# A recurrent attention loop and a long convolution on one core: one arena for the working tiles, a smaller descriptor ring, 13 streamed weight blocks, and loads moved to SyncE

## The chip, the cores and the metric

The kernel runs on one core of a Trainium2 chip. The metric is the device time of one execution, in microseconds; three executions of the kernel before took 2227.32, 2236.9 and 2243.41 us, median 2236.9.

The engines named below are TensorE (PE; its weight loads are PEld), VectorE (DVE), ScalarE (ACT), GpSimd (POOL) and SyncE (SP). SP and POOL also issue DMA transfers, each in its own program order.

## The reference

The output is two halves side by side, 2048 rows each of 1024 columns in bf16.

```python
# half A: 64 segments of 32 rows, one after the other
mem = mem0                                        # [1, 8, 1024]
for s in range(64):
    h = concat([mem, x[:, 32*s:32*s + 32]], 1)    # 40 rows
    q, k, v = (einsum('btd,dhe->bhte', h, W) for W in (Wq, Wk, Wv))   # 32 heads of 128
    scores = einsum('bhqe,bhke->bhqk', q, k) * 128 ** -0.5
    scores = where((idx[:, None] < 8) | (idx[:, None] >= idx[None, :]), scores, -1e9)
    o = einsum('bhqk,bhke->bhqe', softmax(scores), v)
    o = einsum('bhte,hed->btd', o, Wo)
    mem = o[:, :8]                                # carried to the next segment
    outs.append(o[:, 8:])
# half B: a state-space convolution along the 2048 rows
K = einsum('dn,dnl,dn->dl', C, exp(dt * A * l), dt * B).real
y = irfft(rfft(pad(u)) * rfft(pad(K)))[:2048] + u * Dskip
```

The recurrence through `mem` makes the 64 segments of half A sequential. Each needs all of Wq, Wk, Wv and Wo, 64 blocks of 128 x 2048 bf16 (512 KB each), which are more than SBUF holds.

## The kernel before

**Order of the whole.** Half B runs first (0 to about 721 us): tables of powers, spectra of u and of K by matrix products, a pointwise complex product, and inverse products. In its shadow the parts of half A that don't depend on `mem` are projected ahead (keys, queries and values of the 24 rows a segment that come from x alone), kept in DRAM in `PKd`, `PVd` and `XTd`, and weight blocks are loaded into SBUF as rooms come free. Then comes the loop over segments in `part_a` (about 721 to 2150 us), then one product for the left-over rows of all segments, to the end.

**Half B, pointwise stage.** A loop `for b in range(16)` over column quarters `dq = b // 4` and frequency chunks `b % 4`. Each turn does a spectrum of K by matrix products (`spectrum(b + 1)`, L1010), the complex product on DVE (`pointwise(b)`, L1184 to L1195, ten operations), and the issue of the spectrum of u for two turns later (`load_u(b + 2)`, L984, on SP). At b = 0 it also issues `load_k` for the last two quarters (L957): each is 31 small DMAs that gather rows of `Kd`, the key table in DRAM, into `KT2`. From b = 4 on, each turn does two inverse products (L1242) with `load_inverse` (u rows `uu`, L1202) and the store of the result. In the kernel before, POOL issues these key loads, the `uu` loads and the stores.

**A segment.** The state is `hT`, 32 columns for each of eight row groups: 24 from x and 8 from `mem`. Heads are in two halves t = 0, 1. `quads(m, t, kcs)` multiplies `hT` by the blocks of k, q or v (L348), four column groups at once. `evac` copies the result to SBUF on ACT (L354), `tr` transposes it (L359), `scores` makes q times k with the rows of the segment and the 24 rows left of it as two halves of one PSUM tile `sc` of 128 x (2 x 4 x 40). The softmax is two functions over the whole tile, `softmax_a` (largest, subtraction, exponential on ACT) and `softmax_b` (sum, reciprocal, product, two transposes), L389 to L399. `spread` and `spread_l` set the probabilities out in blocks for the next product (`pb`, `lb`, L404 and L407, DVE), and `left_blocks` those of the left rows (`L`, POOL). `pv_x` multiplies v by them; `oproj` (L450) multiplies by the 16 blocks of Wo; `pv_l` is the same product for the left rows. `ob` is the segment's result, half copied by DVE, half by ACT (L540, L541); `tro` transposes it and DVE writes it into `hT` (L546), which releases the next segment.

**Order of work in a segment.** The loop is under `tc.manual_schedule()`: each engine takes its instructions in the order of the text, and waits come from the use of tiles. `between[key]` hangs an extra step (loading `pk`, storing `ob`, fetching a kept block) just before the block `key` is asked for.

**Where weights lie.** Most blocks stay in SBUF (`W_res`). `STREAM` and `STREAM_O` name 14 that `unit` loads afresh in every segment from a DRAM copy `WD` into a ring `wst` of five slots, on SP; a load waits for the matmuls that read the slot last. Two more, (k, 0, 7) and (o, 15), lie in four PSUM banks (`KEPT`, `load_kept`); `fetch` copies them to SBUF in five pieces each with DVE (L283). `SCRATCH` is the SBUF area that holds the ring of descriptors of the DMAs that POOL issues: 2048 bytes a partition; the rest of that area holds `Wlow` blocks.

**Working tiles.** They come from a pool `work` under tags A, B, C, E, F, L and mx; a tag's room is as large as its largest tile, and several tiles share a tag in turn. `pk` (768 wide: kl, ql, vl) and `xt` (192 wide: the next rows of x) are loaded by SP each segment.

Of the kernel before, what the change touches and what calls it, by code (L numbers as in the profile page):

```python
# [24 lines left out]
STREAM = {("k", 0): (1,), ("q", 0): (0, 6), ("k", 1): (3,), ("q", 1): (0, 5), ("v", 0): (2, 7), ("v", 1): (2, 7)}  # L25
STREAM_O = (3, 6, 9, 13)

BANK = {("k", 0): "b0", ("q", 0): "b1", ("k", 1): "b2", ("q", 1): "b0", ("v", 0): "b3", ("v", 1): "b2"}
KEPT = {("k", 0, 7): (("B", 0, 512), ("C", 512, 512), ("A", 1024, 512), ("F", 1536, 256), ("L", 1792, 256)),
        ("o", 15): (("B", 0, 512), ("C", 512, 512), ("E", 1024, 512), ("F", 1536, 256), ("L", 1792, 256))}  # L30
SLOTS = 5

# [33 lines left out]
class Ahead:  # L66
# [3 lines left out]
    def __init__(self, ctx, tc, x, src, seg_len):  # L70
# [5 lines left out]
        self.XTd = dram.tile([self.NS, 128, self.KC * self.XM], BF16, name="XTd")  # L76
        self.PKd = dram.tile([self.NS, 128, 768], BF16, name="PKd")
# [7 lines left out]
    def transposes(self, pool, ps, ident):  # L85
# [7 lines left out]
        for b in range(self.S // 128):  # L93
# [10 lines left out]
            nc.sync.dma_start(out=self.XTd[4 * b:4 * b + 4].rearrange("s p f -> p s f"), in_=xst[:].rearrange("p s k r -> p s (k r)"))  # L104
            yield

    def projections(self):

        nc, KC, NS, XL, PKd, xTl = self.nc, self.KC, self.NS, self.XL, self.PKd, self.xTl
# [13 lines left out]
        def rows_out(t):  # L123
            for k in range(XL):
                late.append(lambda k=k, t=t: nc.sync.dma_start(out=PKd[:].rearrange("s (h k) f -> k s h f", k=XL)[k][:, :, 512 + 128 * t:640 + 128 * t],
                                  in_=self.PVd[t][:].rearrange("(s k) (h e) -> k s h e", k=XL, e=128)[k]))
# [53 lines left out]
def constants(tc, const, ahead):  # L180
# [3 lines left out]
    ident = const.tile([128, 128], BF16, name="a_ident")  # L184
    make_identity(nc, ident[:])
    mask = const.tile([128, 2, NK], BF16, name="mask")
    nc.gpsimd.memset(mask[:], 0.0)
    BD = const.tile([128, 4], BF16, name="BD")
    BDx = ahead.low[2]
    BDL = const.tile([128, 4, 4], BF16, name="BDL")  # L190
# [15 lines left out]
    hT = const.tile([128, ahead.KC, SL], BF16, name="hT")  # L206
# [23 lines left out]
def part_a(ctx, tc, x, src, WD, HE, seg_len, out_a, ahead, W_res, rest, places, first):  # L230
# [13 lines left out]
    XTd, PKd, OLd = ahead.XTd, ahead.PKd, ahead.OLd  # L244
    ident, mask, BD, BDx, BDL, hT = ahead.consts

# [10 lines left out]
    def unit(key):  # L257
# [6 lines left out]
        if key in KEPT:  # L264
            return ahead_of.pop(key)
# [3 lines left out]
        t_ = wst.tile([128, 2048], BF16, name="wst", tag="w%d" % (loads[0] % SLOTS))  # L269
        loads[0] += 1  # L270
        nc.sync.dma_start(out=t_[:], in_=WD[key][:])
        return t_
# [3 lines left out]
    work = ctx_l.enter_context(tc.tile_pool(name="a_work", bufs=1))  # L276
    ps = ctx_l.enter_context(tc.tile_pool(name="a_ps", bufs=1, space=PSUM))
    ps_k = ctx_l.enter_context(tc.tile_pool(name="a_keep", bufs=1, space=PSUM))
    kept, ahead_of = {}, {}
    pn, pt = ahead.low[0:2]  # L280
# [3 lines left out]

    def load_kept(key):
        i = len(kept)
        if key in first:
            t_ = first.pop(key)
        else:
            t_ = wst.tile([128, 2048], BF16, name="wst", tag="w%d" % (loads[0] % SLOTS))  # L290
            loads[0] += 1
            nc.sync.dma_start(out=t_[:].rearrange("e (h d) -> e h d", h=2) if key[0] == "o" else t_[:], in_=src(key))
        kept[key] = [ps_k.tile([128, 512], F32, name="keep", tag="keep%d" % (2 * i + n)) for n in range(2)]
        for n in range(2):
            words(kept[key][n][:], t_[:, 1024 * n:1024 * n + 1024])

    def fetch(key):

        ahead_of[key] = []
        for tag, lo, n in KEPT[key]:  # L300
            t_ = work.tile([128, n], BF16, name="piece", tag=tag)
            words(t_[:], kept[key][lo // 1024][:, lo % 1024 // 2:(lo % 1024 + n) // 2])
            ahead_of[key].append((lo, n, t_))
# [7 lines left out]
    def load_pk(j):  # L311
        pk = pers.tile([128, 768], BF16, name="pk", tag="pk")
        nc.sync.dma_start(out=pk[:], in_=PKd[j])
# [1158 lines left out]
```

## Time and profile before

| what | value |
|---|---|
| median of three executions | 2236.9 us |
| profiled execution, its time | 2233.63 us |
| its span, first to last instruction | 2231.9 us |
| busy: PE, DVE, ACT, POOL | 1908.5, 1400.5, 1025.5, 510.1 us |
| DMA moved | 657.84 MB |
| 63 copies into hT (L546), first and last start | 760.7 and 2136.0 us |

By stage, busy time of each engine with its DMA share and rate:

| stage, us | PE | DVE | ACT | POOL | DMA share | GB/s |
|---|---|---|---|---|---|---|
| half B, tables (0 to 478) | 369.4 | 420.1 | 403.0 | 194.0 | 0.73 | 199 |
| half B, products (478 to 721) | 225.0 | 212.1 | 71.8 | 95.5 | 0.65 | 217 |
| first segment (721 to 761) | 25.1 | 14.9 | 9.6 | 4.0 | 0.96 | 348 |
| the other segments (761 to 2136) | 1211.3 | 737.6 | 526.4 | 201.6 | 0.96 | 350 |
| end (2136 to 2232) | 77.8 | 15.8 | 14.7 | 15.0 | 0.41 | 150 |

How to read what follows. L12 is line 12 of the kernel. A row of a timeline has the start, the duration, engine, line, operation and tiles, and in brackets how long the engine had been idle and what ended that. A row of the table of waits has the total, the number and the longest. A DMA's row on SPq or POOLq is only its issue; the data land later. Busy time on an engine that isn't waited for costs nothing.

### The profile page before, as it was taken

To read this page: it belongs to the slowest core of one execution; us is meant where nothing else is said; L and a number is where in the kernel's file an instruction comes from. 1 tells how busy PE (TensorE), PEld (TensorE's weight loads), DVE (VectorE), ACT (ScalarE), POOL (GpSimd) and SP (SyncE) were. 2 spreads that over 40 slices of the span, in tenths; PEclk is the share of its full clock that TensorE was granted. 3 is DMA by queue.
4 is the path that set the end of the run, shared out by engine and by line. 5 is a ranking of instruction groups with operands and counts; after the bars stand their busy time and mean duration, and the time that the engine had idled before them with its cause. 6 is when DMAs were issued, how large, how long until landed. Compare 5 with 4: busy or idle time off the path is not lost.

```text
span 2231.9 us, 77710 instructions
## 1 busy us (share of the span) xinstructions
PE 1908.5 (86%) x33645; PEld 1181.8 (53%) x33670; DVE 1400.5 (63%) x2904; ACT 1025.5 (46%) x1727; POOL 510.1 (23%) x880
## 2 busy tenths in 40 slices
PE   1599999878999788888888988888889888889879
PEld 1365666657887354554545544544445554544434
DVE  8599999989996455555555545555545554545440
ACT  6699999941333333434343434343334333334330
POOL 2154443566222111111111111111111111111130
PEclk9999999989999899999999999999999999999989
DMA  6877786567458999999999999999999999999981
GB/s 161 195 201 231 220 239 189 158 166 274 151 178 299 342 370 354 355 356 351 359 350 355 361 337 335 359 345 355 342 351 351 362 356 344 344 346 331 362 326 29
DMA packets 351883, 657.84 MB, mean 295 GB/s; under 512 B 118616, under 2 KB 209912, under 8 KB 349492
## 3 DMA queue, kind: packets, MB, share of 16 engines
q1 hardware_dynamic: 336324, 608.69, 78.4%
q0 software_dynamic: 15216, 44.18, 5.8%
q8 instruction: 264, 4.33, 0.8%
q14 instruction: 79, 0.65, 0.1%
HBM read 597.97 MB, written 66.31 MB: 298 GB/s over the span
## 4 chain that ended last, share of the span: by engine, by line
PE 39%; DMA 26%; DVE 17%; issue 10%; ACT 5%; POOL 2%; SPq 2%; ACTq 0%; DVEq 0%; POOLq 0%
PE acc L348 18%; DMA wst<-WD_o 9%; DMA wst<-WD_q 8%; PE pp L450 4%; PE pe L574 2%; DMA wst<-WD_v 2%; PE pro L159 2%; PE tr L359 2%; DVE nr L1071 2%; DMA out_dram<-uu 2%; PE ups L869 2%; PE pa L1040 2%; DMA KT<-Kd 1%; ACT E L1048 1%; DVE mx L395 1%
## 5 line engine op out<-in xcount | busy, mean ns | idle before, releaser
L348 PEld LDWEIGHTS <-hT 128*32 128x32 bf16 x12352 | 341.3, 97 | 331.4 <-issue 103.2
L354 ACT CAST ev<-acc 128x512 bf16<-128x512 f32 x384 | 225.1, 586 | 316.2 <-PE acc L348 310.6
L348 PE MATMUL acc<-W,hT 128*32 128x512 bf16 x4864 | 349.3, 382 | 0.8 <-issue 0.8
L348 PE MATMUL acc<-wst,hT 128*32 128x512 bf16 x2560 | 261.0, 387 | 18.8 <-DMA wst<-WD_q 10.2
L450 PEld LDWEIGHTS <-oT 128*32 128x32 bf16 x8192 | 203.5, 97 | 120.6 <-issue 104.5
L283 DVE TENSOR_SCALAR piece<-keep 128x256 int32<-128x256 int32 (+1 forms) x640 | 189.3, 363 | 93.7 <-PE pp L450 91.9
L366 POOL COPY KT<-pk 128x128 bf16<-128x128 bf16 x128 | 37.6, 294 | 743.3 <-PE acc L348 388.6
L471 DVE COPY KT<-tr 128x512 bf16<-128x512 bf16 x64 | 27.2, 425 | 261.0 <-PE tr L359 261.0
L450 PE MATMUL pp<-W_o,oT 128*32 128x256 bf16 x4096 | 183.9, 277 | 5.1 <-DMA W_o<-in_A_Wo_dram 5.1
L412 POOL TENSOR_TENSOR L<-low_pt,BD 128x128 bf16<-128x128 bf16 x128 | 66.3, 518 | 463.8 <-DVE low_pt L399 236.0
L348 PE MATMUL acc<-MF,hT 128*32 128x512 bf16 x2048 | 170.0, 379 | 0.0
L437 ACT CAST oT<-pv 128x512 bf16<-128x512 f32 x128 | 75.3, 589 | 167.5 <-PE pv L423 167.2
L450 PE MATMUL pp<-wst,oT 128*32 128x256 bf16 x2048 | 102.5, 277 | 37.2 <-DMA wst<-WD_o 36.2
L541 ACT CAST ob<-pp 128x128 bf16<-128x128 f32 x64 | 17.0, 266 | 231.0 <-DVE ob L540 231.0
L159 PE MATMUL pro<-xTl,wsl 128*128 128x512 bf16 x493 | 117.6, 385 | 6.4 <-ACT xTl L103 5.2
L391 ACT ACTIVATE sc<-sc 128x320 f32<-128x320 f32 x128 | 54.0, 422 | 145.4 <-DVE sc L390 115.3
L1010 PEld LDWEIGHTS <-MF 128*128 128x128 bf16 x1024 | 102.4, 100 | 30.9 <-issue 9.8
L389 DVE TENSOR_REDUCE mx<-sc 128x8 f32<-128x320 f32 x128 | 62.2, 486 | 85.9 <-PE sc L382 85.8
L419 PEld LDWEIGHTS <-ev 128*128 128x128 bf16 x1024 | 51.3, 97 | 114.7 <-issue 101.6
L395 DVE TENSOR_REDUCE mx<-sc 128x8 f32<-128x320 f32 x128 | 63.0, 492 | 74.2 <-ACT sc L391 74.2
L1010 PE MATMUL hps<-KT,MF 128*128 128x256 bf16 x720 | 93.8, 282 | 15.7 <-DVE x L1185 12.6
L1242 PE MATMUL yp<-Bt,MI 128*128 128x256 bf16 x680 | 102.8, 273 | 0.8 <-ACT yb L1258 0.8
(315 smaller groups left out, 4011.2 us busy)
## 6 DMA issues: line engine op xcount, KB each, us to landing
wst<-WD_q SPq DMA_DIRECT2D x256, 512.0 KB
wst<-WD_v SPq DMA_DIRECT2D x256, 512.0 KB
wst<-WD_o SPq DMA_DIRECT2D x256, 512.0 KB
wst<-WD_k SPq DMA_DIRECT2D x128, 512.0 KB
Ud<-ux POOLq DMA_DIRECT2D x16, 1024.0 KB, 5.9
uq<-Ud SPq DMA_DIRECT2D x32, 512.0 KB
pk<-PKd SPq DMA_DIRECT2D x64, 192.0 KB
wsl<-in_A_Wk_dram SPq DMA_DIRECT2D x16, 512.0 KB
```

The source lines that it names most:

```text
L159: nc.tensor.matmul(a[:], lhsT=w[:, kc, 128 * j:128 * j + 128], rhs=xTl[:, kc, :, :].rearrange("p s k -> p (s k)"), start=(kc == 0), stop=( ...
L283: nc.vector.tensor_scalar(out=out.bitcast(I32), in0=in_.bitcast(I32), scalar1=0, scalar2=None, op0=ALU.bitwise_or)
L348: nc.tensor.matmul(a[32 * g:32 * g + 32, o_:o_ + rhs.shape[1]], lhsT=hT[:, kc, :], rhs=rhs, start=(kc == 0), stop=(kc == KC - 1), tile_pos ...
L354: nc.scalar.copy(out=q[:], in_=a[:])
L389: nc.vector.tensor_reduce(out=mx[:], in_=sc, axis=AX.X, op=ALU.max)
L391: nc.scalar.activation(out=sc, in_=sc, func=ACT.Exp, scale=scale)
L395: nc.vector.tensor_reduce(out=mx[:], in_=ex, axis=AX.X, op=ALU.add)
L412: nc.gpsimd.tensor_tensor(out=L[:, 0].rearrange("p (a b) k -> p a b k", a=4), in0=bc(S[0][:, 4:8, 0:XL].unsqueeze(2), [128, 4, 4, XL]), in ...
L437: nc.scalar.copy(out=o[:], in_=p[:].rearrange("p a (g q) -> p a g q", g=4))
L450: nc.tensor.matmul(po[32 * qt:32 * qt + 32, :], lhsT=oT[:, h % 4, (h % 16) // 4, :], rhs=columns(w, 1024 * hh + 256 * qt, 256)[0][1], star ...
L1010: pe.matmul(s_[r][half][:, cs, :], lhsT=MF[:, kc, 4 * rr + mc, cs, :], rhs=rhs, start=(i == 0 and mc == 0), stop=(i == 1 and mc == 3), ski ...
L1242: pe.matmul(yp[:, b, :], lhsT=m_[:, b, cs, kc, :], rhs=Bt[:, kc, j, half, c_, :], start=(kc == 0 and cs == 0 and half == 0), stop=(kc == 3 ...
```

## The change

It has five parts.

1. **Weights.** The set of streamed blocks is another, 13 instead of 14. Three blocks are kept in PSUM: (k, 0, 7) whole, (q, 0, 7) and (o, 15) by half, their other halves in SBUF (`HALF`, `halves`, `Whalf`).
2. **Working tiles.** The pool `work` is replaced by one tile `arena` of 5984 bytes a partition; `AT` gives each working tile a byte in it, and `at(name, ...)` a view. `pk` loses `vl` (512 wide); `vx` (448 wide) holds `vl` and the next rows of x. The constants move into the room that the smaller ring leaves.
3. **Program order in a segment.** The softmax is done in the two halves of `sc`, the segment's own rows and those left of it, by `highest`, `below`, `powers` and `norm`. Some steps change places: the scores of t = 0 come after six blocks of k1, and `pv_l(1)` after the copies of `ob`.
4. **Ring.** `SCRATCH` is 512 instead of 2048.
5. **Half B.** The `uu` loads and the 62 DMAs of `load_k` at b = 0 are issued by SP instead of POOL.

```diff
-STREAM = {("k", 0): (1,), ("q", 0): (0, 6), ("k", 1): (3,), ("q", 1): (0, 5), ("v", 0): (2, 7), ("v", 1): (2, 7)}
-STREAM_O = (3, 6, 9, 13)
+STREAM = {("k", 0): (0, 6), ("q", 0): (3,), ("k", 1): (0, 4), ("q", 1): (1, 7), ("v", 0): (3,), ("v", 1): (0, 4)}
+STREAM_O = (0, 5, 10)
-KEPT = {("k", 0, 7): (("B", 0, 512), ("C", 512, 512), ("A", 1024, 512), ("F", 1536, 256), ("L", 1792, 256)),
-        ("o", 15): (("B", 0, 512), ("C", 512, 512), ("E", 1024, 512), ("F", 1536, 256), ("L", 1792, 256))}
+KEPT = {("k", 0, 7): (("K7a", 0, 512), ("K7b", 512, 512), ("K7c", 1024, 512), ("K7d", 1536, 384), (None, 1920, 128)),
+        ("q", 0, 7): (("Q7a", 1024, 512), ("Q7b", 1536, 512)),
+        ("o", 15): (("Oa", 1024, 512), ("Ob", 1536, 384), (None, 1920, 128))}
+HALF = (("q", 0, 7), ("o", 15))
+ARENA = 5984
+AT = {"K7a": 2048, "K7b": 4960, "K7c": 0, "K7d": 3168, "ob": 1024, "pk": 3936, "vx": 0, "Q7a": 4960, "Q7b": 0, "k0": 2048,
...
+    arena = pers.tile([128, ARENA // 2], BF16, name="arena")
+    def at(name, *dims):
+        n = int(np.prod(dims))
+        t_ = arena[:, AT[name] // 2:AT[name] // 2 + n]
...
-        k0 = evac(a, "A")
-        a = quads("q", 0, range(KC))
+        k0 = evac(a, "k0")
+        a = quads("q", 0, range(0, 6))
+        fetch(("q", 0, 7))
+        quads("q", 0, range(6, KC), a)
...
-        tr(p0, 0, k0)
-        tr(p0, 1, q0)
-        nc.vector.tensor_copy(out=KT0[:, :, :, 0:SL], in_=p0[:, 0, :, :, :])
-        nc.scalar.copy(out=QT0[:], in_=p0[:, 1, :, :, :])
-        quads("k", 1, range(3, KC), a)
-        k1 = evac(a, "A")
-        st0, ex0 = softmax_a(scores(0, sc0, QT0, KT0))
+        tr(q0, pq)
+        tr(k0, pk_)
+        nc.scalar.copy(out=QT0, in_=pq[:])
+        nc.vector.tensor_copy(out=KT0[:, :, :, 0:SL], in_=pk_[:])
+        quads("k", 1, range(3, 6), a)
+        scores(0, sc0, QT0, KT0)
+        quads("k", 1, range(6, KC), a)
+        highest(sc0, 0)
+        below(sc0, 0)
+        powers(sc0, 0)
+        highest(sc0, 1)
+        below(sc0, 1)
+        k1 = evac(a, "k1")
+        powers(sc0, 1)
         a = quads("q", 1, range(KC))
+        pt0 = norm(sc0, 0, "pn0", "pt0")
...
+        lt0 = norm(sc0, 1, "ln0", "lt0")
         quads("v", 0, range(2, KC), a)
-        V0 = evac(a, "A")
-        st1, ex1 = softmax_a(scores(1, sc1, QT1, KT1))
+        scores(1, sc1, QT1, KT1)
+        V0 = evac(a, "V0")
+        L0 = left_blocks(lt0, "L0")
+        highest(sc1, 0)
+        below(sc1, 0)
+        powers(sc1, 0)
+        highest(sc1, 1)
...
-        S1 = softmax_b(st1, ex1)
+        pt1 = norm(sc1, 0, "pn1", "pt1")
...
+        below(sc1, 1)
+        powers(sc1, 1)
         oproj(pp[:, 1, :], range(0, 5), o0)
+        pv1 = pv_x(1, V1, pb1, [lb1])
+        o1 = evac_o(pv1, "o1")
+        lt1 = norm(sc1, 1, "ln1", "lt1")
         oproj(pp[:, 1, :], range(5, 8), o0)
-        pv_l(pl_, 1, V1, L1)
-        oproj(pp[:, 1, :], range(8, 14), o1)
+        L1 = left_blocks(lt1, "L1")
         fetch(("o", 15))
-        oproj(pp[:, 1, :], range(14, 16), o1)
+        oproj(pp[:, 1, :], range(8, 16), o1)
         nc.vector.tensor_copy(out=osb[:, 0:128], in_=pp[:, 1, 0:128])
         nc.scalar.copy(out=osb[:, 128:256], in_=pp[:, 1, 128:256])
+        pv_l(pl_, 1, V1, L1)
...
-        gp.dma_start(out=uu[:], in_=u_v[r][:, mc:mc + 2, DQ * dq:DQ * dq + DQ])
+        sy.dma_start(out=uu[:], in_=u_v[r][:, mc:mc + 2, DQ * dq:DQ * dq + DQ])
...
-            ks += [load_k(DQ * i, DQ, (gp,), KT2[i - 2]) for i in (2, 3)]
+            ks += [load_k(DQ * i, DQ, (sy,), KT2[i - 2]) for i in (2, 3)]
...
-SCRATCH = 2048
+SCRATCH = 512
```

The new softmax functions, `i` being the half:

```python
def highest(sc, i):
    nc.vector.tensor_reduce(out=mx[:, 4 * i:4 * i + 4], in_=sc[:, i], axis=AX.X, op=ALU.max)
def below(sc, i):
    nc.vector.tensor_tensor(out=sc[:, i], in0=sc[:, i], in1=bc(mx[:, 4 * i:4 * i + 4].unsqueeze(2), [128, 4, NK]), op=ALU.subtract)
def powers(sc, i):
    nc.scalar.activation(out=sc[:, i], in_=sc[:, i], func=ACT.Exp, scale=scale)
def norm(sc, i, pn, pt):
    m_ = mx[:, 4 * i:4 * i + 4]
    nc.vector.tensor_reduce(out=m_, in_=sc[:, i], axis=AX.X, op=ALU.add)
    nc.vector.reciprocal(out=m_, in_=m_)
    pn, pt = at(pn, 4, NK), at(pt, 5, SL)
    nc.vector.tensor_tensor(out=pn, in0=sc[:, i], in1=bc(m_.unsqueeze(2), [128, 4, NK]), op=ALU.mult)
    nc.vector.transpose(out=pt[:, 0:4, :], in_=pn[:, :, 0:SL])
    nc.vector.transpose(out=pt[:, 4:5, :], in_=pn[:, :, SL:NK])
    return pt
```

## The prediction

> **What bounds the kernel now.** I read the windows first, because shares over the whole span mix two parts with different limits. The columns are each engine's busy time, then the TensorE clock, the DMA share and GB/s.
>
> ```profile
> 505.00:515.00 10.00, 6.72 (x47) 5.18 (x45) 9.03 (x8) 1.14 (x3) 7.06 (x13) 0.84 1.05 369
> 525.00:535.00 10.00, 10.00 (x94) 8.97 (x92) 9.04 (x8) 2.08 (x6) 6.85 (x13) 1.00 0.99 337
> ...
> 1000.00:1500.00 500.00, 438.82 (x9539) 247.88 (x9534) 265.71 (x717) 191.07 (x384) 72.02 (x156) 0.99 0.96 351
> 1500.00:2000.00 500.00, 439.70 (x9569) 248.93 (x9566) 269.64 (x724) 190.90 (x382) 74.17 (x159) 0.99 0.96 350
> ```
>
> Part B's pointwise stage (about 478 to 525) keeps DVE over 90% busy with PE waiting for it; from 525 PE is full. In the segment loop PE is 88% busy and DMA 96%. The 63 hT copies (L546) run from 760.7 to 2136.0, so 1375.3/62 = 22.18 us a segment.
>
> Next, what PE waits for between 1000 and 2000 us, 45 segments:
>
> ```profile
> PE pp L450 <- DMA wst<-WD_o: 26.6, 39, 2.3
> PE tro L545 <- DVE ob L540: 20.1, 45, 0.5
> PE pv L419 <- DVE pk L404: 18.5, 35, 0.8
> PE acc L348 <- DVE hT L546: 16.5, 44, 0.4
> PE pv L423 <- DVE lb L407: 12.6, 39, 0.3
> ```
>
> With wst_q (8.3), wst_v (2.6) and wst_k (0.7), streamed blocks cost 38.2/45 = 0.85 us a segment, DVE's softmax chain (pk, lb) 0.69, and the tail (tro, hT) 0.81. So the loop has two limits close together, DMA and a chain DVE-PE-ACT. Removing one uncovers the other. The timeline of DVE in one segment gives the chain:
>
> ```profile
> 1430.49 0.49 DVE L389 TENSOR_REDUCE mx<-sc 128x8 f32<-128x320 f32 x1 [1.23 <-PE sc L382]
> 1431.02 0.50 DVE L390 TENSOR_TENSOR sc<-sc,mx 128x320 f32<-128x320 f32 x1
> 1432.09 0.49 DVE L395 TENSOR_REDUCE mx<-sc 128x8 f32<-128x320 f32 x1 [0.57 <-ACT sc L391]
> ...
> 1439.21 0.89 DVE L407 TENSOR_TENSOR lb<-low_pt,BDL 128x512 bf16<-128x512 bf16 x1
> ```
>
> First mx to the end of lb takes 9.6 us, all DVE but two waits of 0.57 us for the exponential. hT (1423.45) to mx is 7.0. After lb come its matmul and the oT copy (0.9), 8 output blocks at 0.31 (24 matmuls of L450 take 0.92 in the chain of this segment), then ob, ob, tro, hT (1.0): 4.4. With no late block a segment costs 7.0 + 9.6 + 4.4 = 21.0, close to the shortest seen, 20.87.
>
> **The Trainium skill.** "DMA: Bandwidth & Descriptors", Specifications, gives about 358 GB/s of HBM for a core: the loop's 350 at 0.96 agrees, so it is near what DMA can give. Its section "Issuing engines are not separate DMA queues" says that moving a DMA to another engine saves only time on the sequencer. I use the reverse: the issue time doesn't vanish, it is paid on SP. The trace shows that price on both engines (below). "Anatomy of one DMA — SWDGE (gpsimd) path" of that page says that DMA engines don't wait for semaphores, the issuing sequencer does, so whatever stands behind a DMA on SP waits with it; the 157 us that SP stands at L318 for PE agree. "VectorE: DVE Perf Modes", section on the TRN2 errata, says that an operation on SBUF operands pays a fixed extra cost, so many small tiles pay it per tile. Here the operands lie in PSUM, which it doesn't price, but the trace shows such a cost there too: 292 ns for 128 f32 elements from PSUM (L540) and 490 for 320, hence 1.03 ns an element and 160 ns fixed.
>
> **The change part by part.**
>
> *13 blocks for 14, PKd/VXd for PKd/XTd.* Bytes a segment: before 14 x 0.524 + pk 0.197 + xt 0.049 + stores 0.131 = 7.72 MB; after 13 x 0.524 + 0.131 + vx 0.115 + 0.131 = 7.19, 6.8% less. At 350 GB/s that is 20.5 us, below 22.18. Gain by itself: between 0.85 (all block waits) and 22.18 - 20.5 = 1.6 us a segment, if nothing else binds.
>
> *Softmax in halves* (L389 to L399 become highest, below, powers, norm for 4 rows of heads each). 14 DVE operations become 28. At 160 elements a reduce, subtract or multiply costs 160 + 165 = 0.33, 0.35 with spacing; the transposes about 0.28 and 0.16, the reciprocal 0.20: norm 1.34. The exponential falls from 0.42 to about 0.29, with its hop 0.45. The two halves share a PSUM tile that is tracked whole, so highest of the second half waits for powers of the first. From the first highest: 2 x (0.35 + 0.35 + 0.45) = 2.30; norm 3.64; pb0, lb0 (0.45, 0.65, 0.27) 5.0; second norm 6.35; highest, below, powers and highest again for t = 1 7.85; norm 9.2; pb1 and lb1 (0.43, 0.85) 10.5. Before: 9.6. Halving moves the left rows of t = 1 (below, powers, norm) behind lb1, which takes work off the chain, yet 14 more fixed costs put 0.9 on it. DVE busy a segment goes from 11.9 to about 14.
>
> *Scores of t = 0 after six k1 blocks instead of eight*: -2 x 0.24 = -0.45 before mx (7.0 to 6.55); the three blocks left (0.72) cover the KT copy (0.42 and a hop).
>
> *pv_l(1) behind the ob copies*: it writes the tile pp that ACT's ob copy reads, so it starts after that, and tro stands behind it on PE. 5 short matmuls, 0.35 to 0.5: tail 4.4 to 4.9. Bounds 0.2 and 0.6.
>
> *Pieces, half-blocks, vx, arena*: k 7 costs DVE the same 2048 columns, q 7 and o 15 1024 each, as o 15 did; they lie in DVE's idle time before mx and before ob (3.8 and 1.3 us in that segment). If that cover went, q 7 would cost its 0.75. Arena places are reused once their last reader is through; one more matmul and load each on PE, 0.05. L0 and L1 on POOL (0.52 + 0.70) end before PE needs them.
>
> Loop sum: 6.55 + 10.5 + 4.9 = 21.95 with no late block, and 20.5 for DMA, so few late blocks: 22.1, with 21.3 and 22.5 as ends (each price 10% off, the hop between halves hidden or not). Against 22.18 x 63 that is -5 us (-55 to +20). The gain from DMA goes into the chain.
>
> *Key loads on SP.* load_k for i = 2, 3 is 62 DMAs (L957), on POOL in before, beside everything. On SP the program puts them after the Dsk load and ahead of load_u(2).
>
> ```profile
> 437.98 12.50 SPq L957 DMA_DIRECT2D KT<-Kd  x16
> ...
> 497.12 1.34 SPq L1163 DMA_DIRECT2D Dsk<-in_B_Dskip_dram  x1
> 498.57 1.31 SPq L984 DMA_DIRECT2D uq<-Ud  x2
> ```
> ```profile
> 505.83 1.23 DVE L1189 TENSOR_TENSOR y<-uq,x 128x1024 f32<-128x1024 f32 x1 [1.25 <-DMA uq<-Ud]
> ```
> ```profile
> 532.51 0.55 POOL L957 DMA_DIRECT2D KT<-Kd  x1 [0.36 <-issue]
> 533.05 3.54 POOL L1202 DMA_DIRECT2D uu<-in_B_u_dram  x5
> ```
>
> Already before, the pointwise product of b = 2 waits 1.25 us for uq. SP issued 16 such loads in 12.5 us, 0.78 each with hitches, median 0.60; POOL took 0.72 (488.45 to 533.05). 62 x 0.65 = 40 us between Dsk and uq. uq then lands near 546 instead of 505.8 and DVE stands for it. The order on DVE and PE is fixed, PE has no backlog there (67% busy), and afterwards DVE, then PE, are full, so nothing gives it back: +40. Lower bound 62 x 0.36 = 22 less a few us, say 18; upper 62 x 0.78 = 48. The keys themselves aren't read before b = 6, and MI and the later uq come behind uq(2) and are in time for the shifted work. The uu loads on SP (0.7 each) wait for stores on which DVE's own progress depends: 0 to +5, I take 0; POOL gets rid of 40 us of issuing that nobody waited for.
>
> *Ring of 512 B*: what POOL still issues is few and small; 0 to +5, taken 0. First segment: one half-block more to hold ready, 0.5 MB at 350 GB/s: +1.5.
>
> **Sum** against the profiled execution's 2233.6 (0.15% below the median of 2236.9; its span is 2231.9): 2233.6 + 40 + 1.5 - 5 = 2270.
>
> **The rivals.** About 1%, 22 us, is what a measurement of this kernel can tell from no change.
>
> *Faster: the loop follows DMA.* For it: the DMA share of 0.96 and 0.85 us of block waits. Against: the 21.0 floor of the chain, to which the halves add. If the chain's additions are hidden (second-half operations slip into the 0.57 us waits), the segment is 20.5 to 21.3, -55 to -103 us; with the queue's +40, 2165 to 2215, middle 2195. It decides where a segment is under 21.2.
>
> *No change: the key loads are cheap or covered*, 62 x 0.36 less slack, or a small gain of the loop pays for them. For: the best spacing on SP is well under POOL's. 2233.6 + 18 - 15 = about 2237 (2215 to 2257).
>
> *Much slower*: halves cost 0.4 us a segment more than summed because the arena's reuse or POOL's L blocks hold PE. 2270 + 25 and more, over 2315.
>
> *The change doesn't do what it says*: a segment still shows a DMA share of 0.96 and block waits, since it moves bytes earlier, not fewer. The byte count excludes it.
>
> **Numbers.** Forecast 0.51 (2257 to 2315), faster rival 0.26, no change 0.19, much slower 0.04. The range leaves out the fast half of the first rival and the last one: 2193 to 2316. The forecast's own is 2257 to 2315.
>
> **What would show it.** uq on DVE at b = 2 with a wait of tens of us; KT<-Kd on SP between 498 and about 538, POOL free there; the end of part B later by it. In the loop: hT period near 22.1, DVE busy near 14 us a segment, wst waits of PE nearly gone, pv waits on DVE larger, DMA share about 0.9. A period under 21.3, or part B unshifted, makes the prediction wrong.

## The result and the profile after

The changed kernel takes 2213.4 us (median of four executions, 2206.8 to 2217.4) against 2236.0 us for the kernel before: ratio 0.990, 95% interval 0.985 to 0.994. The prediction was 2270 us and slower. The kernel became faster, by more than the interval. The time does lie inside the wide range of 2193 to 2316, but on the other side of the kernel before, and below the 2257 at which the forecast's own range begins.

The profiled execution has a span of 2211.4 us, 20.5 less than before. Four stages give and take (times of a stage's end: the last start of the inverse product in half B, and the first and last copy into hT):

| stage | before | after | change | forecast |
|---|---|---|---|---|
| half B, to its last inverse product | 718.3 | 753.1 | +34.8 | +40 |
| from there to the first copy into hT | 42.4 | 56.0 | +13.6 | +1.5 |
| 62 segments between first and last copy | 1375.3 | 1297.7 | -77.6 | -5 |
| from the last copy to the end | 95.9 | 104.6 | +8.7 | 0 |

So 77.6 us were won in the loop and 57.1 given back around it. Of the losses only the first had been priced near its size.

Half B does what was forecast. This is the timeline of SP, and under it that of DVE, of the changed kernel:

```profile
496.40 38.96 SPq L986 DMA_DIRECT2D KT<-Kd  x62
535.47 1.00 SPq L1013 DMA_DIRECT2D uq<-Ud  x2
```
```profile
539.92 1.22 DVE L1218 TENSOR_TENSOR y<-uq,x 128x1024 f32<-128x1024 f32 x1 [35.95 <-DMA uq<-Ud]
```

62 key loads at 0.63 us stand between Dsk and uq, and DVE idles 35.95 us where it had waited 1.25.

At the start of the loop there is a second queue on SP, which the forecast took for harmless:

```profile
711.38 25.45 SPq L1231 DMA_DIRECT2D uu<-in_B_u_dram  x5
736.88 0.47 SPq L229 DMA_DIRECT2D W<-in_A_Wq_dram  x1
```

Five uu loads take SP 25 us. What SP waits for there is stores (`out_dram<-uu`, up to 9.7 us each); weight blocks that the loop needs are issued after them. In windows of 20 us, the DMA share is 0.25 from 720 to 740 and 1.01 from 740 to 760.

At the end, POOL's issuing has changed. Its timeline in the last segment, where it loads seven blocks of OLd:

```profile
2117.16 1.70 POOL L520 DMA_DIRECT2D Wlow<-OLd  x3 [0.22 <-issue]
2126.12 0.53 POOL L520 DMA_DIRECT2D W_k<-OLd  x1 [7.25 <-issue]
2128.62 0.53 POOL L520 DMA_DIRECT2D W_k<-OLd  x1 [1.97 <-issue]
...
```

Before, the seven were issued in 3.8 us without a pause; now POOL sits idle between them with no releaser to be seen, and PE's wait for POOL's L behind them grows from 12.0 to 21.6 us.

In the loop, a segment takes 1297.7/62 = 20.93 us instead of 22.18. One of the windows (columns as in the prediction) and what PE waits for between 1000 and 2000 us (about 48 segments) follow. In the changed kernel most working tiles are views of `arena`, so the rows name that:

```profile
1000.00:1500.00 500.00, 448.95 (x10196) 261.81 (x10188) 312.98 (x1104) 209.93 (x456) 60.17 (x168) 1.00 0.97 348
```
```profile
PE pp L433 <- ACT arena L569: 36.8, 47, 0.8
PE acc L364 <- DMA wst<-WD_q: 13.5, 23, 1.8
...
PE acc L364 <- DMA wst<-WD_v: 7.9, 8, 1.4
...
PE pp L463 <- DMA wst<-WD_o: 0.7, 2, 0.5
PE pv L437 <- DVE arena L421: 0.3, 1, 0.3
```

Waits for streamed blocks fell from 0.85 to 0.46 us a segment, those for DVE's softmax chain (0.69) to almost nothing. The new wait of 0.78 is `pv_l(1)` behind ACT's copy of ob. DVE is busy 13.1 us a segment instead of 11.9, yet its chain has not grown where no wait stretches it. Some rows of DVE in one segment:

```profile
1423.37 0.33 DVE L398 TENSOR_REDUCE a_mx<-sc 128x4 f32<-128x160 f32 x1 [0.70 <-PE sc L393]
...
1424.49 0.32 DVE L398 TENSOR_REDUCE a_mx<-sc 128x4 f32<-128x160 f32 x1 [0.44 <-ACT sc L404]
...
1426.97 0.43 DVE L418 TENSOR_TENSOR arena<-arena,a_BDx 128x512 bf16<-128x512 bf16 x1
...
1432.29 0.69 DVE L421 TENSOR_TENSOR arena<-arena,a_BDL 128x512 bf16<-128x512 bf16 x1
...
1437.33 0.19 DVE L575 COPY a_hT<-tro 128x64 bf16<-128x64 bf16 x1 [0.89 <-PE tro L574]
```

From the first highest to the end of lb1 it is 9.6 us, as before; the forecast had 10.5. The half operations cost what was worked out (0.33), and the second half does wait for ACT: taken from start to start in this segment and in the one that the prediction shows, the steps of the softmax took 6.95 us before and take 7.57. But the products that set out pb and lb took 2.66 and take 2.04 (lb1 0.69 for 0.89), which gives the 0.62 back.

### The profile page after: what moved, and what is told of

Same layout as the page of the kernel before. It is cut to its first block, busy times and chain, and to the rows that moved or that the text cites. A ratio compares the mean times of both kernels' runs of the same rounds, so it can differ in the third digit from the quotient of the medians.

```text
span 2211.4 us, 79458 instructions
## 1 busy us (share of the span) xinstructions
PE 1868.7 (85%) x33734; PEld 1176.6 (53%) x33734; DVE 1474.9 (67%) x3800; ACT 1041.9 (47%) x1855; POOL 407.6 (18%) x786
## 4 chain that ended last, share of the span: by engine, by line
PE 33%; DMA 13%; DVE 11%; issue 4%; ACT 3%; POOL 1%; ACTq 0%; SPq 0%; DVEq 0%; POOLq 0%
PE acc L364 16%; PE pp L463 9%; DMA wst<-WD_q 6%; DMA wst<-WD_v 4%; PE pe L603 2%; DVE arena L421 2%; PE tr L375 2%; DMA wst<-WD_o 1%; DVE arena L411 1%; PE pv L437 1%; DVE a_mx L398 1%; DVE a_mx L408 1%; ACT sc L404 1%; ACT arena L370 1%; DMA W_o<-in_A_Wo_dram 1%
## 5 line engine op out<-in xcount | busy, mean ns | idle before, releaser
L364 PEld LDWEIGHTS <-a_hT 128*32 128x32 bf16 x12352 | 321.9, 96 | 343.8 <-issue 69.1
L370 ACT CAST arena<-acc 128x512 bf16<-128x512 f32 x384 | 225.3, 587 | 329.5 <-PE acc L364 284.9
L364 PE MATMUL acc<-W,a_hT 128*32 128x512 bf16 x4608 | 359.4, 381 | 0.0
L364 PE MATMUL acc<-wst,a_hT 128*32 128x512 bf16 x2560 | 258.9, 385 | 49.7 <-DVE a_hT L575 17.9
L463 PEld LDWEIGHTS <-arena 128*32 128x32 bf16 x8256 | 215.6, 97 | 82.9 <-issue 52.5
L292 DVE TENSOR_SCALAR arena<-keep 128x256 int32<-128x256 int32 (+1 forms) x512 | 175.6, 395 | 47.4 <-PE acc L364 43.5
L364 PE MATMUL acc<-MF,a_hT 128*32 128x512 bf16 x2048 | 183.6, 382 | 0.0
L463 PE MATMUL pp<-W_o,arena 128*32 128x256 bf16 x4096 | 145.3, 275 | 8.0 <-DMA W_o<-in_A_Wo_dram 6.0
L398 DVE TENSOR_REDUCE a_mx<-sc 128x4 f32<-128x160 f32 x256 | 80.8, 316 | 105.5 <-ACT sc L404 56.0
L433 PEld LDWEIGHTS <-arena 128*128 128x128 bf16 x1024 | 54.8, 97 | 138.4 <-ACT arena L569 61.4
L408 DVE TENSOR_REDUCE a_mx<-sc 128x4 f32<-128x160 f32 x256 | 82.0, 320 | 50.4 <-ACT sc L404 50.4
L375 PEld LDWEIGHTS <-arena 128*128 128x128 bf16 x1024 | 57.9, 98 | 77.7 <-ACT arena L370 46.0
```

The lines of the kernel that those rows point to most:

```text
L292: nc.vector.tensor_scalar(out=out.bitcast(I32), in0=in_.bitcast(I32), scalar1=0, scalar2=None, op0=ALU.bitwise_or)
L364: nc.tensor.matmul(a[32 * g:32 * g + 32, o_:o_ + rhs.shape[1]], lhsT=hT[:, kc, :], rhs=rhs, start=(kc == 0), stop=(kc == KC - 1), tile_pos ...
L370: nc.scalar.copy(out=q, in_=a[:])
L375: nc.tensor.transpose(out=p[:, hl, :, :].rearrange("p a b -> p (a b)"), in_=q[:, 128 * hl:128 * hl + 128], identity=ident[:])
L398: nc.vector.tensor_reduce(out=mx[:, 4 * i:4 * i + 4], in_=sc[:, i], axis=AX.X, op=ALU.max)
L408: nc.vector.tensor_reduce(out=m_, in_=sc[:, i], axis=AX.X, op=ALU.add)
```

## The experiments

For each kernel I take the mean segment from the first and last copy into hT, and the shortest segment and the shortest values of its three parts from DVE's rows, leaving out the first five segments: from the copy into hT to where the wait for the first scores ends (mx), from there to the end of lb1 (lb), from there to the next copy. The shortest segment shows the chain without late blocks; what the mean has over it I call lateness. Before, that is 1.31 us, after it 0.49; so of the 1.25 us that a segment gained, 0.43 is a shorter floor and 0.82 less lateness. A segment is that of the one profiled execution. In kernels with the same loop the mean agrees within 0.08 us (20.89 to 20.97 in four kernels with the changed loop), so smaller differences say nothing. Where the number of loads differs from the kernel's own, a block is put in another's place: the work stays the same, the output is not the reference's.

| kernel | mean segment | shortest | hT to mx, mx to lb, lb to hT, shortest | median time, us |
|---|---|---|---|---|
| before | 22.18 | 20.87 | 6.80, 9.67, 4.39 | 2236 |
| after | 20.93 | 20.44 | 6.45, 9.67, 4.32 | 2213 |
| before, 13 loads | 21.52 | 20.86 | 6.80, 9.59, 4.39 | 2189 |
| after, 14 loads | 21.28 | 20.44 | 6.45, 9.66, 4.32 | 2227 |
| after, 12 loads | 20.82 | 20.44 | 6.45, 9.66, 4.32 | 2207 |
| before, scores after six | 22.41 | 21.28 | 6.80, 9.51, 4.39 | 2245 |
| before, q0 first and scores after six | 22.19 | 20.60 | 6.38, 9.71, 4.39 | 2233 |
| after, scores after eight | 21.07 | 20.83 | 6.84, 9.67, 4.32 | 2227 |
| before, after's choice of blocks | 22.49 | 20.87 | 6.80, 9.47, 4.39 | 2237 |
| before, room for xt | 21.74 | 20.87 | 6.80, 9.67, 4.39 | 2199 |
| before, xt + q0 first + 13 loads | 21.15 | 20.49 | 6.38, 9.51, 4.39 | 2164 |
| after, POOL product beside lb1 | 20.98 | 20.65 | 6.45, 9.88, 4.32 | 2222 |
| after, shorter chain | 20.90 | 20.19 | 6.45, 9.06, 4.68 | 2209 |
| after, shorter chain and three costs undone | 20.88 | 20.19 | 6.45, 9.06, 4.68 | 2161 |

### Half B: the key loads alone, and undone

```diff
-            ks += [load_k(DQ * i, DQ, (gp,), KT2[i - 2]) for i in (2, 3)]
+            ks += [load_k(DQ * i, DQ, (sy,), KT2[i - 2]) for i in (2, 3)]
```

> Kernel before, with one part of the change alone: the 62 key loads at b = 0 issued by SP. Theory (the SP queue holds up uq(2), nothing gives it back): the wait of DVE for uq grows from 1.25 to about 36 us, part B and the end come 35 us later, the loop keeps 22.18 us a segment: about 2271 us, ratio 1.016. Rival (part of the delay is slack that later stages take up, and the loss in the changed kernel has another cause): under 2255 us, ratio below 1.008.

Measured: ratio 1.017 (1.014 to 1.021). The kernel before, with this line alone changed:

```profile
499.57 38.99 SPq L957 DMA_DIRECT2D KT<-Kd  x62
```
```profile
543.00 1.23 DVE L1189 TENSOR_TENSOR y<-uq,x 128x1024 f32<-128x1024 f32 x1 [37.88 <-DMA uq<-Ud]
```

The loop stays at 22.2 us. The line costs what the queue says, and nothing gives it back.

The other way round, the changed kernel with this line undone:

> Changed kernel with the key loads back on POOL, ring still 512 B. Theory: part B ends 35 us earlier, loop unchanged at 20.9 us: about 2213 - 35 = 2178 us. Rival (the small ring makes POOL's issue of 62 gathers slow, so that the keys come late and stand in the way there): POOL's issue of the 62 grows from 45 us to 80 and more, and the gain is under 20 us: 2195 or more.

Measured: 2179.1 us, ratio to the kernel before 0.976 (0.973 to 0.980). The first copy into hT comes at 773.8 instead of 809.1. POOL needs 53 us for the 62 with short pauses, but nobody waits for them. The move to SP was worth 34 us of loss, and the ring of 512 bytes did not force it.

### The uu loads, and the ring

```diff
-        sy.dma_start(out=uu[:], in_=u_v[r][:, mc:mc + 2, DQ * dq:DQ * dq + DQ])
+        gp.dma_start(out=uu[:], in_=u_v[r][:, mc:mc + 2, DQ * dq:DQ * dq + DQ])
```

> Changed kernel with only the uu loads back on POOL. Theory (on SP they wait for output stores and hold up the weight loads behind them, which stretches the start of the loop by 13.6 us): the gap in DMA at 720 to 737 us goes, the first copy into hT comes 10 to 13 us earlier: about 2201 us. Rival (the longer start is the cost of loading the half blocks and of other places for the blocks, not of the queue): 2210 or more.

Measured: 2240.0 us (ratio to before 1.004), 27 us more than the changed kernel. The theory was wrong. The time lies in the rival's range (2210 or more), but no view had foreseen a loss. POOL's timeline shows it:

```profile
579.67 0.73 POOL L1231 DMA_DIRECT2D uu<-in_B_u_dram  x1 [1.80 <-issue]
...
586.97 0.73 POOL L1231 DMA_DIRECT2D uu<-in_B_u_dram  x1 [3.59 <-issue]
```

With the small ring all 32 of these loads, and 15 of the 32 stores, are preceded by 1.8 to 7.5 us in which POOL waits for nothing that the profile names. Loads and stores on one such queue don't keep up with the inverse products: half B ends 16 us later than in the changed kernel and the first copy into hT comes 25.6 later. So this run doesn't isolate what the uu loads on SP cost, and it leaves the rival open, that half-blocks and other places of blocks make the start longer; it shows that on SP these loads are the smaller evil beside this ring.

The keys and the uu loads both on POOL, and OLd on SP:

```diff
-                nc.gpsimd.dma_start(out=raw[j][:], in_=OLd[j])
+                nc.sync.dma_start(out=raw[j][:], in_=OLd[j])
```

> Changed kernel with keys and uu loads back on POOL, and the seven OLd loads of the last segment moved from POOL to SP. Theory (the three costs add up: 35 + 12 + 9): about 2157 us, and PE's wait for POOL in the last segment falls from 21.6 to about 12 us or less. Rival (they overlap, so that undoing one uncovers another): 2175 or more.

Measured: 2215.2 us (0.993), so the gains don't add, as the rival had it (2175 or more). It carries the uu loss: half B ends at 763 us, 45 later than with the keys alone on POOL. But its end, from the last copy into hT, takes 88.8 us instead of 104.6: seven OLd loads on SP are worth 16 us.

```diff
-SCRATCH = 2048
+SCRATCH = 512
```

> Kernel before with the descriptor ring at 512 bytes instead of 2048, all else as before. Theory (with the small ring a POOL transfer of 128 or 256 rows is issued only when the one before it has drained, 2 to 7 us; this is what drives the uu loads off POOL and lengthens the last segment): part B about 16 us longer, the start of the loop 10 later, PE's wait for POOL in the last segment 22 instead of 12 us: about 2265 us. Rival (the ring is harmless, a cost of 0 to 5 us): under 2240 us.

Measured: 2302.1 us, ratio 1.032 (1.021 to 1.043). The kernel before loses 65 us up to the first copy into hT and 4 at the end, with its loop unchanged (22.19 us). The direction was right and the size more than double. The ring is not harmless: with it, the uu loads can't stay beside the stores on POOL without this loss, and on SP they stand in front of something. Of the end it explains only a part. In two kernels with the end of the kernel before, that part takes 95.9 (before) and 92.4 us (its keys on SP); with the small ring 99.5, in the changed kernel 104.6. What the rest comes from is open.

### Is the loop bound by bytes?

```diff
+        if key == ("o", 8) and loads[0] > 2 * SLOTS + 20:
+            return stage(key, WD["o", 5][:])
         if key in W_res:
```

> Changed kernel with one transfer of 512 KB more in each segment: block (o, 8), resident before, is replaced by a fresh load of another block, 14 loads again (the product uses that other block, so the output isn't the reference's). Theory (DMA sets the segment, before and after): 7.72 MB a segment, 20.93 x 7.72 / 7.19 = 22.4 us, about 2305 us in all. Rival (after the change the chain DVE-PE-ACT sets it, DMA has room): at most 21.3 us a segment, under 2240 us.

Measured: 21.28 us a segment, not 22.4, and that in an execution 8 us above the median. One of its windows, in the columns of the windows above:

```profile
1500.00:2000.00 500.00, 447.96 (x10108) 261.07 (x10103) 310.61 (x1096) 207.20 (x452) 59.31 (x168) 1.00 1.00 368
```

14 loads pass at 366 GB/s on the mean of both windows. So the 350 GB/s of the kernel before, with a DMA share of 0.96, was no ceiling, and the measurement is above the 358 GB/s too, which the prediction takes from the Trainium skill, "DMA: Bandwidth & Descriptors", Specifications. Some of the transfers of the kernel before were asked for too late.

```diff
         between.pop(key, lambda: None)()
+        if key == ("o", 5) and loads[0] > 2 * SLOTS + 20:
+            return W_res["o", 7]
```

> Changed kernel with one load less in each segment: block (o, 5) is taken from a resident block instead, 12 loads (the product uses that other block, so the output isn't the reference's). Theory (DMA sets the segment at 20.93, the chain of 6.5 + 9.6 + 4.35 = 20.5 stands close behind it): 20.5 us, about 2187 us, with a DMA share below 0.93. Rival A (DMA alone matters): 20.93 x 6.67 / 7.19 = 19.4 us. Rival B (the chain sets it already): 20.9 us.

Measured: 20.82. Neither bytes alone nor the chain alone: one block less saves 0.11, one more costs 0.35. The changed kernel stands near where both limits meet.

```diff
         between.pop(key, lambda: None)()
+        if key == ("o", 9) and loads[0] > 2 * SLOTS + 20:
+            return W_res["o", 7]
```

> Kernel before with one load less in each segment: block (o, 9) is taken from a resident block, 13 loads, all else as before (the product uses that other block, so the output isn't the reference's). Theory (the whole gain of the loop is the bytes; halves, arena and order are neutral): 20.9 to 21.2 us a segment against 22.18. Rival (the new softmax and order are needed for the gain): 21.6 us or more.

Measured: 21.52. Half of the gain (0.66 of 1.25) comes with one block less; the rest needs another part of the change. At equal loads the changed kernel is 0.6 (13) to 0.9 us (14) shorter.

### Which other part: the scores, the blocks, or a wait in SP's queue

```diff
-        quads("k", 1, range(3, KC), a)
-        k1 = evac(a, "A")
-        st0, ex0 = softmax_a(scores(0, sc0, QT0, KT0))
+        quads("k", 1, range(3, 6), a)
+        scores(0, sc0, QT0, KT0)
+        quads("k", 1, range(6, KC), a)
+        k1 = evac(a, "A")
+        st0, ex0 = softmax_a(sc0[:].rearrange("p a b k -> p (a b) k"))
```

> Kernel before, with the scores of t = 0 after six blocks of k1 instead of eight, all else as before. Theory (this is the part of the new order that shortens the loop's floor): hT to mx 6.80 to about 6.45 at its shortest, a segment 21.8 to 22.0 us instead of 22.18, about 2220 us. Rival (late blocks take it up): 22.1 us or more.

Measured: 22.41 us, slower (1.008, 1.006 to 1.011), and the shortest hT to mx stays at 6.80. PE now waits for ACT's copy of QT (L473, 16.4 us in 44 times between 1000 and 2000 us), because q0 is transposed behind k0.

With q0 ahead of k0 and each in its own bank, as in the changed kernel, and the scores after six as above:

```diff
-        p0 = new_tr("b3")
-        tr(p0, 0, k0)
-        tr(p0, 1, q0)
+        pq, p0 = new_tr("b0"), new_tr("b3")
+        tr(pq, 0, q0)
+        tr(p0, 0, k0)
...
```

> Kernel before with q0 transposed first, q0 and k0 into PSUM banks of their own, and the scores of t = 0 after six blocks of k1. Theory (scores earlier shorten hT to mx only if ACT's copy of q0 starts before k0 is transposed, which the earlier attempt left out): hT to mx 6.45 at its shortest against 6.80, floor of a segment 20.5 instead of 20.87; the mean falls by 0.2 or more, to below 22.0, if late blocks leave it. Rival (with 14 blocks the late ones take it up): shortest 6.45, mean still 22.1 or more.

Measured: hT to mx 6.38, and a mean of 22.19. The floor falls and the mean doesn't: late blocks take it up. The reverse, in the changed kernel:

```diff
-        quads("k", 1, range(3, 6), a)
+        quads("k", 1, range(3, KC), a)
         scores(0, sc0, QT0, KT0)
-        quads("k", 1, range(6, KC), a)
```

> Changed kernel with the scores of t = 0 after all eight blocks of k1 again. Theory (the 0.35 us by which hT to mx is shorter, is worth its size in the changed kernel's loop): hT to mx 6.9, a segment 21.2 us instead of 20.93. Rival (slack towards the transfers takes it up): 20.9 to 21.0 us.

Measured: the floor rises by 0.39, the mean by 0.14.

Next the choice of streamed blocks, with the hooks of pk, the stores and the kept block moved to the nearest streamed block:

```diff
-STREAM = {("k", 0): (1,), ("q", 0): (0, 6), ("k", 1): (3,), ("q", 1): (0, 5), ("v", 0): (2, 7), ("v", 1): (2, 7)}
-STREAM_O = (3, 6, 9, 13)
+STREAM = {("k", 0): (0, 6), ("q", 0): (3,), ("k", 1): (0, 4), ("q", 1): (1, 7), ("v", 0): (3,), ("v", 1): (0, 4)}
+STREAM_O = (0, 5, 9, 12)
```

> Kernel before with the changed kernel's choice of streamed blocks, still 14: k, q and v as in the changed kernel, of o blocks 0, 5, 9 and 12; the small loads hang on the nearest streamed block. Theory (which blocks are streamed decides how late they are; in the kernel before the ones of o arrive late, 0.6 us a segment): waits for wst_o fall, a segment 21.3 to 21.7 us against 22.18. Rival (lateness is a matter of bytes alone): 22.1 us or more.

Measured: 22.49 in the profiled execution, the time of the whole the same (1.001, 0.996 to 1.005). The choice alone does not make it better; SP stands at the load of xt for PE longer (3.8 us a segment for 2.5).

That wait was the last candidate. In the kernel before, xt shares the room of tag F with `lb0b`, which PE's product reads. SP runs ahead, reaches the load of xt early, and holds the loads of blocks behind it.

```diff
-        xt = work.tile([128, KC, XM], BF16, name="xt", tag="F")
+        xt = ahead.low[3]
...
-... for name, n, m in (("pn", 8, 40), ("pt", 10, 32), ("BDx", 4, 32))])
+... for name, n, m in (("pn", 8, 40), ("pt", 10, 32), ("BDx", 4, 32), ("xt", 8, 24))])
```

> Kernel before with a room of its own for xt (384 bytes left over beside the small tiles), so that its load no longer waits for PE's product with lb0b, which shared its room; all else as before, 14 blocks. Theory (SP stands 2.5 us a segment at the xt load, with loads of blocks queued behind it, and these come late): that wait is gone, wst_o waits of PE fall below 0.3 us a segment, a segment 21.4 to 21.8 us against 22.18. Rival (the queue has slack there; bytes alone make blocks late): 22.0 us or more.

Measured: 21.74 us a segment, ratio 0.984 (0.975 to 0.993). The waits of PE between 1000 and 2000 us:

```profile
PE acc L348 <- DMA wst<-WD_q: 17.1, 28, 2.0
...
PE pp L450 <- DMA wst<-WD_o: 2.9, 6, 1.1
```

Waits for blocks of o fall from 26.6 to 2.9 us with the same bytes; some come back as waits for q. DMA moves 358 GB/s on the mean of both windows. SP's wait at the load of xt falls from 2.5 to 0.3 us a segment.

> Kernel before with three parts put together: xt in its own room, q0 transposed first with scores after six blocks, and 13 loads (block (o, 9) from a resident one, so that the output isn't the reference's). If these three make the changed kernel's loop, a segment takes 20.8 to 21.1 us with whole softmax, no arena and no new set of streamed blocks. Rival (something else of the change is needed): 21.3 us or more.

Measured: 21.15, a little above what was expected. The diff is the sum of the three above (xt, q0 first with scores after six, 13 loads). Three small parts put into the kernel before, with its whole softmax and its pool, give 1.03 of the 1.25 us. The last 0.2 is open. As a whole this kernel takes 2164 us, 49 less than the changed one, because it has none of the three costs outside the loop.

### The chain: POOL beside DVE, and a shorter softmax

```diff
+        left_blocks(pt1, "aside")
         spread(pb1, pt1[:, 0:4, :])
...
```

> Changed kernel with one more left_blocks on POOL for t = 1, on the segment's own rows, whose result nobody reads: it runs beside pb1 and lb1 on DVE, as POOL's L did before the change. Theory (DVE's products of two bf16 operands in SBUF are slowed by a POOL product that runs at the same time, which is why pb0 took 0.63 and lb1 0.89 before and 0.43 and 0.69 after): pb1 goes from 0.42 to about 0.6, lb1 from 0.69 to about 0.9, the chain grows by 0.3 to 0.4 us, a segment is 21.1 to 21.3. Rival (the difference is the place in memory or the number of operands in line): durations as in the changed kernel, 20.9 us.

The groups of the changed kernel between 1000 and 2000 us, then those of this kernel:

```profile
L418 DVE TENSOR_TENSOR arena<-arena,a_BDx 128x512 bf16<-128x512 bf16 x96 | 41.3, 430 | 1.6
L421 POOL TENSOR_TENSOR arena<-arena,a_BDL 128x128 bf16<-128x128 bf16 x96 | 38.3, 399 | 0.0
...
L421 DVE TENSOR_TENSOR arena<-arena,a_BDL 128x512 bf16<-128x512 bf16 x48 | 33.1, 690 | 0.1
```
```profile
L421 POOL TENSOR_TENSOR arena<-arena,a_BDL 128x128 bf16<-128x128 bf16 x143 | 78.1, 546 | 0.0
...
L421 DVE TENSOR_TENSOR arena<-arena,a_BDL 128x512 bf16<-128x512 bf16 x47 | 41.7, 887 | 0.0
L418 DVE TENSOR_TENSOR arena<-arena,a_BDx 128x512 bf16<-128x512 bf16 x95 | 40.9, 430 | 1.6
```

lb1 goes from 690 to 887 ns, which is its 883 ns in the kernel before, and POOL's own product from 399 to 546. pb1 stays at 430, where the theory had 0.6. The chain grows by 0.21, not by 0.3 to 0.4; the segment's 0.05 can't be told from none.

Why pb1 is spared can be read in the kernel before, from POOL's and DVE's rows for pb0 and pb1 (which lies in the room of pk):

```profile
1433.90 0.40 POOL L412 TENSOR_TENSOR L<-low_pt,BD 128x128 bf16<-128x128 bf16 x1 [3.10 <-DVE low_pt L398]
1438.91 0.64 POOL L412 TENSOR_TENSOR L<-low_pt,BD 128x128 bf16<-128x128 bf16 x1 [4.07 <-DVE low_pt L399]
```
```profile
1433.95 0.63 DVE L404 TENSOR_TENSOR pb<-low_pt,low_BDx 128x512 bf16<-128x512 bf16 x1
1438.87 0.42 DVE L404 TENSOR_TENSOR pk<-low_pt,low_BDx 128x512 bf16<-128x512 bf16 x1
```

The one that starts second pays. For pb0 POOL is first by 0.05 us: POOL takes its 0.40, DVE 0.63 instead of 0.42. For pb1 DVE is first by 0.04, and POOL takes 0.64. For pb0 this holds in 57 of the 60 segments between 800 and 2130 us; in the other three POOL's product is nearly over when pb0 starts, which then takes 0.43 to 0.49. In the kernel with the added product pb1 starts 0.1 us ahead of POOL, so POOL pays; in one segment, at 996 us, POOL was first, and there pb1 took 0.60.

This agrees with the Trainium skill, "SBUF — State Buffer", which says in its list under the diagram that a DVE operation with two SBUF operands and a GpSimd one contend for one pair of ports, that the first to start gets it, and that the other fully blocks. The delay in the rows, 0.21 us for pb0, is shorter than the 0.35 us by which the two overlap.

So halving moved POOL's L out of the time of pb and lb: L of t = 0 now runs beside the operations of t = 1 on PSUM, L of t = 1 beside the copies of block (o, 15) out of PSUM. That paid for the added fixed costs.

```diff
-        highest(sc0, 0)
-        below(sc0, 0)
-        powers(sc0, 0)
-        highest(sc0, 1)
-        below(sc0, 1)
+        nc.vector.tensor_reduce(out=mx[:], in_=w0, axis=AX.X, op=ALU.max)
+        nc.vector.tensor_tensor(out=w0, in0=w0, in1=bc(mx[:].unsqueeze(2), [128, 8, NK]), op=ALU.subtract)
         k1 = evac(a, "k1")
-        powers(sc0, 1)
+        nc.scalar.activation(out=w0, in_=w0, func=ACT.Exp, scale=scale)
...
-        highest(sc1, 1)
...
+        highest(sc1, 1)
         below(sc1, 1)
```

> Changed kernel with two steps of its softmax set otherwise: for t = 0 the largest, the subtraction and the exponential go over the whole tile again (one of each in place of two), and for t = 1 the largest of the left rows is taken after lb1. Theory (the chain DVE-ACT from first highest to lb1, 9.67 us at its shortest, sets the segment together with late blocks): the chain gets 0.7 + 0.3 us shorter, about 8.7 us; a segment 20.2 to 20.4 us instead of 20.9, so 2165 to 2180 us. Rival (transfers alone set the segment): 20.8 us or more, 2205 or more.

Measured: the chain is 9.06 at its shortest, the tail grows to 4.68 (PE now waits for ACT's copy of o1), the floor falls by 0.25; the mean stays at 20.90. The rival's range holds: with the changed kernel's loads, this much off the floor buys nothing that can be measured.

### A version that beats both

The kernel with the shorter chain, with the key loads on POOL and the OLd loads on SP as above, and in the last turns of half B the weight loads ahead of `inverses(1)`:

```diff
     for n_ in range(8):
-        inverses(1)
         for _ in range((10, 5)[n_] if n_ < 2 else 1):
             next(resident, None)
+        inverses(1)
```

> The same softmax, and of the changed kernel's costs outside the loop: key loads back on POOL (-35), the seven OLd loads of the last segment on SP (-16), uu loads still on SP but behind the last weight loads of half B instead of ahead of them (-5). If the gains add: about 2213 - 45 - 35 - 16 - 5 = 2112 us. If SP's waits for uu only move: 2125 or more.

Measured: 2161.5 us (2160.3 to 2162.5), ratio to the kernel before 0.970 (0.967 to 0.973). Keys (34) and OLd (16) paid. The exchange of `inverses(1)` and weight loads paid nothing: the first copy into hT follows half B's end by 57.9 us, as in the kernel with only the keys undone (56.0), since four uu loads of the turns before it still hold SP for 21.8 us. The softmax paid nothing either.

## Why the prediction was right or wrong

The step that failed is the loop's sum, 6.55 + 10.5 + 4.9 = 21.95 us for a segment without late blocks. The runs show 6.45 + 9.67 + 4.32 = 20.44. That the measured time still lies between 2193 and 2316 is luck: losses of 21 us that nobody had priced stand against a gain that was forecast 73 us too small, and without them the time would be 2192.

**Key loads on SP, +40**: right in mechanism, place and size. 35.95 us of wait, 0.63 us each, nothing given back; alone it makes the kernel before 1.7% slower.

**Loop, -5**: wrong, -77.6. The first term held; the other two were too large.

- The chain, 10.5: measured 9.67 at its shortest, as before. The fixed costs of the halves were about right (7.84 us of softmax steps forecast, 7.57 in the segment shown). Mis-sized were the products that set out pb and lb: 1.37 us for pb0 and lb0 and 1.28 for pb1 and lb1, measured 1.01 and 1.03. The forecast took them from the rows of before, where they were slowed by POOL's L running beside them, and did not ask where L would run after the change. The run with the added product shows this for lb1, the rows of before for pb0.
- The tail, 4.9: measured 4.32, less than the 4.39 before. `pv_l(1)` behind ob lengthens the wait of DVE's hT copy from 0.68 to 0.89, so there it costs 0.2, the lower bound. But the forecast only added it and did not take it away from where it had stood, between two groups of oproj, where its matmuls held the chain of the kernel before for 0.27 us:

```profile
1420.25 0.20 PE pp L419 x4
1420.45 0.07 PE pp L423
```

The gain from fewer late blocks was there: the forecast put it at 0.85 us or more "if nothing else binds", and lateness fell by 0.82. It was lost in the forecast because the chain and the tail were to grow by as much.

A part of it came about otherwise than forecast. "At 350 GB/s" took the rate of before as the ceiling and lateness as a matter of bytes. The text even cited that SP stands at L318 for PE 157 us, and then priced the move of that small load at nothing. Its room was the largest single part next to the block: -0.44 us a segment, 27 us in all, with no byte saved. The vx of the changed kernel has SP waiting 0.7 us in place of 2.5.

**uu loads on SP, 0 to +5, taken 0**: the reason given, that DVE's own progress depends on the same stores, looked only at who waits for uu. Queued behind them are weights that the first segments need. That this makes the 13.6 us at the start is argued from SP's timeline and the gap in DMA, not shown; no run isolated it, since the ring spoiled the one that was meant to.

**Ring, 0 to +5, taken 0**: wrong. With everything left on POOL it costs 66 us, nearly all before the loop; in the changed kernel it is a part of the 8.7 us at the end.

**Rivals**: the faster one came true in its condition (a segment under 21.2) and its loop gain (-55 to -103); its total of 2165 to 2215 just holds the result, because the start and the end took 21 us that no case had. (By its own terms, 2233.6 + 40 + 1.5 less 55 to 103, that total is 2172 to 2220.) Its reason, that the chain's additions would be hidden, was not what happened: the additions were there and the products got shorter. The forecast of slower rested on the 10.5 and the 4.9.

## What to carry to other kernels

A small load with a waiting destination, in the middle of a queue of large ones, makes the large ones late: before blaming the bytes, look at what the issuing engine waits for and give that load a room of its own. When transfers are moved between queues, list what stands behind them on the new queue, not only who waits for them. Durations taken from rows of an engine that shares ports with another hold only while the same neighbour runs beside it and starts in the same order. When a step moves to another place in the chain, count it out where it stood as well as in where it goes.

## What the runs showed of the hardware

- With a descriptor ring of 512 bytes a partition, POOL's uu loads (256 rows of 512 bytes) are each preceded by a pause of 1.8 to 7.5 us with no releaser; at 2048 bytes the pauses without a releaser before the same loads are 0.3 us in all. Three transfers of 128 rows of 4 KB are issued at once, and the fourth waits 7.25 us; at 2048 bytes seven were issued in 3.8 us.
- A core streamed 366 GB/s over 1000 us with a DMA share of 0.99 to 1.00, above the 350 that looked like a limit at 0.96. A DMA share of 0.96 was not a full queue.
- A DVE product of two bf16 operands in SBUF of 128x512 (lb1) takes 690 ns alone and 887 when a POOL product already runs; another of the same size (pb) takes 0.63 us when POOL is first and 0.42 when DVE is. POOL's own product of 128x128 takes 0.40 us alone or first, and 0.46 to 0.95 when it starts inside a product of DVE.
